# Pooled attention followed by a four-expert attention mixture: q loaded by partition groups and turned by VectorE, first scores on 32-row tiles, and a new written-out order

## The chip, the cores and the metric

The kernel runs on one core of one Trainium2 chip. The metric is the device time of one execution in microseconds; lower is better. Each time of the kernel before is one execution, and the median of three is given.

## What is computed

Inputs are q, k and v of shape 8 batches x 8 heads x 576 positions x 64, and the weights of four experts. Per batch:

```python
k_p = k.reshape(B, H, 72, 8, D).mean(axis=3)         # pooled by 8: 72 keys
v_p = v.reshape(B, H, 72, 8, D).mean(axis=3)
attn = softmax(q @ k_p.T / sqrt(D)); x = attn @ v_p   # first attention, 8 heads
x = x.transpose(0, 2, 1, 3).reshape(B, S, H * D)      # 576 x 512
logits = x @ w_gate                                   # gate: top 2 of 4 experts
for e in range(4):                                    # second attention, causal
    a = causal_softmax((x @ wq[e]) @ (x @ wk[e]).T / sqrt(64))
    out += gate_weight[e] * (a @ (x @ wv[e]) @ wo[e])
```

## The kernel before, in words

The work of a batch is cut into small steps with one- or two-letter names, and a string SEQ (from L551) lists about a thousand of them in one hand-off order: `name args:batch@bank`, with a trailing `d` where the copy that follows a matrix step runs on VectorE instead of ScalarE, and a trailing `c` where a 128-column stationary operand is cut into four strips of 32 columns (`wide`, `flip`, `strips`, L181 to L194). Each engine runs its own steps strictly in the order of the string. There is no scheduler behind it: a step waits only for its data and for its PSUM bank. PSUM is one tile of 8 banks, and the `@` figure is the bank, fixed in the string.

The steps of the first attention, for batch b:

- `L_k`, `L_q`, `L_v` (`load`, L109): DMAs issued from GpSimd, which cast fp32 to bf16 on the way. k and v come in three chunks each, q in six chunks of 96 positions for all 8 heads, 96 partitions per DMA with runs of 64 elements. There are three buffers of each (NRAW).
- `PK`, `kc`, `KT`, `kt`: pooling of k by a matmul with a 0 and 1/8 matrix, its copy, four PE transposes of 96x128 and their copy, so that kpT holds two heads of 64 rows on the 128 partitions.
- `Q0` to `Q3`, `r0` to `r3` (L246, L251): q is turned by PE transposes. Each Q step flips six 96x128 pieces of two heads into one bank as 128x576 bf16 (line L194), and r copies the bank to the tile qT (line L176). A batch has 24 flips and 4 copies.
- `E0` to `E4`, `e0` to `e4` (L255, L263): the scores. E0 to E3 are two matmuls each, one per head, with 64 rows of the array each and 512 columns, into two adjacent banks; E4 does the last 64 positions of all heads. e is the exp on ScalarE, 96x1024 for a pair of banks (L273).
- `D`, `d`, `x` and `PV`, `vc`, `O`, `o`: sums of the exps by a matmul with ones, their reciprocal as exp(-ln(.)) on ScalarE (L294, L298), pooled v, the weighted sum, and its scaling on VectorE into xT (L317).

The second part, two batches to a tile xT: `P` and `p` are the q and k projections of the experts, with their copies; `V` and `v` the values with the gate logits; `g` the gate; `S` and `s` the scores (64-row tiles, two banks) and their exp (L433); `a` the causal mask on GpSimd (L450); `B`, `bz`, `bg`, `b` the weighted sum, its normalizing and gating; `T` and `t` its PE transposes and copy; `Y` and `y` the output projection, its copy and the DMA out. `span` (L456) says into how many parts B is cut: two for batches 0 to 5, three for the last two.

`W0` to `W4` load the expert weights, `c0` to `c4` put them in order; in the string W0 stands behind the loads of batch 1's k and q. `H` steps are matmuls on zeros (L173) that keep TensorE busy while there is nothing to do; there are 51 of them. `M` sets pads on VectorE.

The loads stand in one FIFO on GpSimd together with the causal masks. The copies of all steps are written by one helper (line L176), nearly all matmuls by another (line L185), and so groups are told apart by their tiles.

TensorE addresses its array in tiles: 128x128 for P, V, B, T, Y and the flips, 64x128 for E and S (two matmuls side by side), 128x32 for PK, PV, D, O and the steps with a `c` (four side by side). Going along the string, the tile shape of TensorE changes 97 times; 80 of the changes come behind the first `P_q0:0`.

Of the kernel before, what the change touches and what calls it, by code (L numbers as in the profile page):

```python
# [21 lines left out]
def kernel(  # L22
# [34 lines left out]
    NQC = S // KR  # L57
# [16 lines left out]
    qraws = bufs(NRAW, [KR, NQC, H, D], BF16, "qraw")  # L74
# [3 lines left out]
    kpTs = bufs(2, [128, NHP, KR], BF16, "kpT")  # L78
    vps = bufs(2, [KR, H, D], BF16, "vp")
    qTs = bufs(8, [128, S], BF16, "qT")  # L80
    etas = bufs(2, [KR, NHP, 2, S], BF16, "eta")
# [27 lines left out]
    def load(b, nm, c):  # L109
        if nm == "q":  # L110
            dst = qraws[b % NRAW][:, c, :, :]
            src = q[b, :, KR * c : KR * (c + 1), :].rearrange("h p d -> p h d")
        else:
            raw, T = (kraws, k) if nm == "k" else (vraws, v)
            dst = raw[b % NRAW][:, c, :, :, :].rearrange("p h t d -> p h (t d)")
            src = T[b, :, 2 * KR * c : 2 * KR * (c + 1), :].rearrange("h (p t) d -> p h (t d)", t=2)
        nc.gpsimd.dma_start(out=dst, in_=src)  # L117
# [107 lines left out]
    def kc(b, bank, dve):  # L225
        copy(dve, kps[b % 2][:], psum[0:KR, bank, :])
# [10 lines left out]
    def KT(b, bank):  # L237
        for hp in range(NHP):
            flip(half_bank(bank)[:, KR * hp : KR * hp + KR],
                 kps[b % 2][:, 128 * hp : 128 * hp + 128])  # L240

    def kt(b, bank, dve):
        copy(dve, kpTs[b % 2][:],
             half_bank(bank)[:, 0 : NHP * KR].rearrange("p (a n) -> p a n", a=NHP))
# [18 lines left out]
    def es(b, bank, dve, hp):  # L263
        eta = etas[b % 2]
        if hp == NHP:
            for hh in range(2):
                nc.scalar.activation(
                    out=eta[:, :, hh, MAIN:S],
                    in_=psum[0:KR, bank + hh, 0 : NHP * TAIL].rearrange("p (a n) -> p a n", a=NHP),
                    func=EXP, scale=ATT_EXP_SCALE,  # L270
                )
        else:
            nc.scalar.activation(  # L273
                out=eta[:, hp, :, 0:MAIN], in_=psum[0:KR, bank : bank + 2, :],
# [3 lines left out]
    def heads(b, g, cols):  # L278
        for i in range(4):
            yield i, 4 * g + i, etas[b % 2][:, 2 * g + i // 2, i % 2, cols]  # L280
# [175 lines left out]
    def span(b, part):  # L456
        if b < B - 2:
# [78 lines left out]
    def z(b, c, queue):  # L536
# [9 lines left out]
    MATRIX = {"PK": PK, "PV": PV, "KT": KT, "Q": Q, "E": Es, "D": Dn, "O": Ov, "V": V, "P": P,  # L546
              "S": Sb, "B": Bv, "T": T, "Y": Y}
    READS = {"kc": (kc, "PK"), "vc": (vc, "PV"), "kt": (kt, "KT"), "r": (r, "Q"), "e": (es, "E"),
# [3 lines left out]
        I:0 L_k0:0 L_k1:0 L_k2:0 J:0 K:0 H19:0@0 PK:0@0 kc:0 H4:0@1 KT:0@0 kt:0 L_q0:0 L_q1:0  # L552
        L_q2:0 L_q3:0 L_q4:0 L_q5:0 H8:0@1 Q2:0@0 r2:0 Q1:0@1 Q3:0@2 r1:0d r3:0 H1:0@3 E2:0@4
        e2:0 Q0:0@1 r0:0 E3:0@2 H5:0@0 E0:0@4 e3:0 L_v0:0 L_v1:0 E4:0@0 L_v2:0 PV:0@6 vc:0d e4:0
# [150 lines left out]
```

## Time and profile before

| what | us |
|---|---|
| median of 3 runs (range) | 167.88 (167.41 to 168.09) |
| span of the profiled execution, first to last instruction | 165.0 |
| median less that span | 2.88 |
| TensorE busy | 157.0 |
| ScalarE busy | 135.0 |
| VectorE busy | 123.8 |
| GpSimd busy, most of it issuing DMAs | 104.9 |

The profiled execution is known by its span alone; what the metric holds beside it (2.88 us) is taken as the same for both kernels. Busy times are unions of instruction spans. A matmul's span includes its way through the array, so that a TensorE that always has the next one in flight shows as busy throughout; the columns that it streams are worked out from starts that follow each other. Instructions of ScalarE and VectorE overlap at their ends by about 0.1 us, so a group's cost on the engine is the distance of the starts, not the mean duration.

### The profile page before, as it was taken

To read this page: it belongs to the slowest core of one execution; us is meant where nothing else is said; L and a number is where in the kernel's file an instruction comes from. 1 tells how busy PE (TensorE), PEld (TensorE's weight loads), DVE (VectorE), ACT (ScalarE), POOL (GpSimd) and SP (SyncE) were. 2 spreads that over 40 slices of the span, in tenths; PEclk is the share of its full clock that TensorE was granted. 3 is DMA by queue.
4 is the path that set the end of the run, shared out by engine and by line. 5 is a ranking of instruction groups with operands and counts; after the bars stand their busy time and mean duration, and the time that the engine had idled before them with its cause. 6 is when DMAs were issued, how large, how long until landed. Compare 5 with 4: busy or idle time off the path is not lost. (4 is left out here: it accounts for less than half of the span.)

```text
span 165.0 us, 6106 instructions
## 1 busy us (share of the span) xinstructions
PE 157.0 (95%) x2463; PEld 93.8 (57%) x2463; DVE 123.8 (75%) x410; ACT 135.0 (82%) x247; POOL 104.9 (64%) x178
## 2 busy tenths in 40 slices
PE   6999988999999999999999999999999999999980
PEld 2344354568557656654754878555647686555730
DVE  1101497589799859976988899998998989779960
ACT  3029758999998999888998997789997999898860
POOL 6999891899999999965959997400140211364100
PEclk9999999999999999999999999999999999999998
DMA  2999999999999999999999999923113043055875
GB/s 22 160 153 171 164 172 178 170 145 139 177 156 173 164 157 148 156 233 217 206 178 226 168 198 83 174 100 86 47 68 127 4 131 127 0 190 195 257 260 191
DMA packets 84204, 25.04 MB, mean 152 GB/s; under 512 B 79312, under 2 KB 79568, under 8 KB 84176
## 3 DMA queue, kind: packets, MB, share of 16 engines
q0 software_dynamic: 78928, 15.21, 110.6%
q1 hardware_dynamic: 5024, 9.05, 15.9%
q8 instruction: 19, 0.31, 0.7%
q10 hardware_dynamic: 224, 0.39, 0.6%
q14 instruction: 9, 0.07, 0.1%
HBM read 30.42 MB, written 9.44 MB: 242 GB/s over the span
## 5 line engine op out<-in xcount | busy, mean ns | idle before, releaser
L433 ACT ACTIVATE etb_97<-psum 128x1024 bf16<-128x1024 f32 x24 | 23.6, 1023 | 2.5 <-PE psum L185 2.4
L433 ACT ACTIVATE etb_98<-psum 128x1024 bf16<-128x1024 f32 x24 | 23.5, 1027 | 1.3 <-PE psum L185 1.1
L450 POOL TENSOR_SCALAR_AFFINE_SELECT etb_98<-etb_98 128x256 bf16<-128x256 bf16 x32 | 12.5, 410 | 17.4 <-ACT etb_98 L433 17.2
L450 POOL TENSOR_SCALAR_AFFINE_SELECT etb_97<-etb_97 128x256 bf16<-128x256 bf16 x32 | 12.4, 415 | 15.8 <-ACT etb_97 L433 15.7
L173 PE MATMUL psum<-warm 128*128 128x512 bf16 x51 | 15.2, 443 | 1.8 <-DVE onesd L146 1.3
L273 ACT ACTIVATE eta_91<-psum 96x1024 bf16<-96x1024 f32 x16 | 15.9, 1018 | 1.1 <-PE psum L185 1.1
L273 ACT ACTIVATE eta_92<-psum 96x1024 bf16<-96x1024 f32 x16 | 15.6, 1020 | 0.7 <-PE psum L185 0.6
L117 POOL DMA_DIRECT2D qraw_68<-in_q_dram x18 | 13.9, 775 | 1.2 <-PE psum L185 1.1
L176 DVE COPY ofin<-psum 128x512 f32<-128x512 f32 (+1 forms) x18 | 11.9, 673 | 3.2 <-PE psum L185 2.4
L117 POOL DMA_DIRECT2D qraw_69<-in_q_dram x18 | 13.8, 770 | 0.5 <-issue 0.5
L176 DVE CAST qk_99<-psum 128x512 bf16<-128x512 f32 (+1 forms) x16 | 10.5, 670 | 3.8 <-PE psum L185 3.6
L176 DVE CAST qk_100<-psum 128x512 bf16<-128x512 f32 (+1 forms) x16 | 10.5, 654 | 3.5 <-PE psum L185 3.5
L176 ACT COPY ofin<-psum 128x512 f32<-128x512 f32 (+1 forms) x19 | 10.7, 580 | 2.7 <-PE psum L185 1.8
L185 PE MATMUL psum<-wvg,xT_96 128*32 128x260 bf16 (+1 forms) x120 | 10.8, 275 | 0.0
L173 PEld LDWEIGHTS <-warm 128*128 128x128 bf16 x51 | 5.1, 111 | 9.5 <-issue 5.8
L185 PE MATMUL psum<-wvg,xT_95 128*32 128x260 bf16 (+1 forms) x156 | 10.5, 275 | 0.0
L185 PEld LDWEIGHTS <-etb_97 128*128 128x128 bf16 x240 | 8.8, 97 | 2.0 <-issue 0.4
L117 POOL DMA_DIRECT2D qraw_70<-in_q_dram x12 | 9.2, 784 | 0.0
L185 PEld LDWEIGHTS <-etb_98 128*128 128x128 bf16 x240 | 8.3, 97 | 1.4 <-issue 0.8
L185 PE MATMUL psum<-qk_100 64*128 64x64 bf16 (+4 forms) x96 | 8.8, 276 | 0.1
L117 POOL DMA_DIRECT2D kraw_71<-in_k_dram x9 | 7.0, 787 | 2.7 <-DMA qraw_70<-in_q_dram 1.8
L185 PE MATMUL psum<-qk_99 64*128 64x64 bf16 (+4 forms) x96 | 8.4, 277 | 0.0
(198 smaller groups left out, 452.8 us busy)
## 6 DMA issues: line engine op xcount, KB each, us to landing
out_dram<-ofin SPq DMA_DIRECT2D x31, 256.0 KB, 3.0
kraw_71<-in_k_dram POOLq DMA_DIRECT2D x9, 192.0 KB, 6.2
qraw_68<-in_q_dram POOLq DMA_DIRECT2D x18, 96.0 KB, 5.3
vraw_74<-in_v_dram POOLq DMA_DIRECT2D x9, 192.0 KB, 5.5
kraw_72<-in_k_dram POOLq DMA_DIRECT2D x9, 192.0 KB, 5.9
qraw_69<-in_q_dram POOLq DMA_DIRECT2D x18, 96.0 KB, 5.5
vraw_75<-in_v_dram POOLq DMA_DIRECT2D x9, 192.0 KB, 4.9
kraw_73<-in_k_dram POOLq DMA_DIRECT2D x6, 192.0 KB, 6.5
```

What stands on the lines that cost most here:

```text
L117: nc.gpsimd.dma_start(out=dst, in_=src)
L173: nc.tensor.matmul(out=psum[:, bank, :], lhsT=warm[:, 0:128], rhs=warm[:], start=True, stop=True)
L176: (nc.vector.tensor_copy if dve else nc.scalar.copy)(out=out, in_=in_)
L185: nc.tensor.matmul(out=out, lhsT=lhsT, rhs=rhs, start=start, stop=stop)
L273: nc.scalar.activation(out=eta[:, hp, :, 0:MAIN], in_=psum[0:KR, bank : bank + 2, :], func=EXP, scale=ATT_EXP_SCALE,)
L433: nc.scalar.activation(out=et[:, ep, :, eo : eo + n], in_=psum[:, bank : bank + 2, 0:n], func=EXP, scale=MOE_EXP_SCALE,)
L450: nc.gpsimd.affine_select(out=blk, in_=blk, pattern=[[0, 2], [1, 128]], compare_op=ISGE, fill=0.0, base=0, channel_multiplier=-1,)
```

## The change

- q of one batch is loaded by four DMAs, each to 32 partitions: partition group i takes heads 2i and 2i+1 (g = 0, 1), a partition holds pairs of neighbouring positions, and the runs are 128 elements long. For batch 0 each is cut in two by g, so eight DMAs, and those of g = 0 come first.
- The Q and r steps are gone. `u0` and `u1` (`turn`) turn q by a VectorE transpose of 32x32 blocks, SBUF to SBUF, on pairs of bf16 seen as one fp32: 128x576 such pairs in one instruction, two instructions per batch. After it a partition group of 32 holds one head of the group, a partition holds two neighbouring elements of the head's 64, and the two stand next to each other for each position.
- The scores E are made on tiles of 32 rows and 128 columns: for g = 0 and 1, four heads side by side into four banks, in two accumulating passes (the even and the odd elements), the moving operand read with a step of two elements. E0 and E1 are the 512 columns of g = 0 and 1, E2 the rest of both. An E step now takes two pairs of banks (`E0:0@02` is banks 0 to 3), and two exps of the same size as before follow it (`e00`, `e01`). k is pooled and flipped with its columns reordered to match.
- `span` cuts B into three parts for the first two batches too: 40 B steps for 36, 32 T steps for 24.
- No step has a `c` any more. The tile shape changes 114 times along the string, 105 of them behind the first `P_q0:0`, and 34 warm-up matmuls are left of 51.
- The string is new. The first two weight loads stand behind batch 0's v, ahead of batch 1's loads; batch 0's projections come ahead of batch 1's scores. More copies run on ScalarE (5 weight orderings for 1, 14 p for 8, 14 t for 3, 23 y for 18; fewer of kt, 2 for 5, v, 11 for 14, and kc, 4 for 5).

The core of the diff:

```diff
-    qraws = bufs(NRAW, [KR, NQC, H, D], BF16, "qraw")
+    qraws = bufs(NRAW, [128, 2, NQB, 2, D], BF16, "qraw")
...
-    def load(b, nm, c):
+    def load(b, nm, c, g=None):
         if nm == "q":
-            dst = qraws[b % NRAW][:, c, :, :]
-            src = q[b, :, KR * c : KR * (c + 1), :].rearrange("h p d -> p h d")
+            i, gs = c, slice(0, 2) if g is None else slice(g, g + 1)
+            dst = qraws[b % NRAW][32 * i : 32 * i + 32, gs].rearrange("p g a t d -> p g a (t d)")
+            src = q[b].rearrange("(i g) (a p t) d -> i p g a (t d)", g=2, a=NQB, t=2)[i][:, gs]
...
     def KT(b, bank):
-        for hp in range(NHP):
-            flip(half_bank(bank)[:, KR * hp : KR * hp + KR],
-                 kps[b % 2][:, 128 * hp : 128 * hp + 128])
+        for j in range(4):
+            g, par = j // 2, j % 2
+            flip(half_bank(bank)[:, KR * j : KR * j + KR],
+                 kps[b % 2][:, 256 * g + par : 256 * g + 256 : 2])
...
-    def Q(b, bank, hp):
-        for c in range(NQC):
-            flip(half_bank(bank)[:, KR * c : KR * (c + 1)],
-                 qraws[b % NRAW][:, c, 2 * hp : 2 * hp + 2, :].rearrange("p h d -> p (h d)"))
-
-    def r(b, bank, dve, hp):
-        copy(dve, qTs[4 * (b % 2) + hp][:], half_bank(bank)[:, 0:S])
+    def turn(b, g):
+        src = qraws[b % NRAW][:, g].rearrange("p a t d -> p (a t d)").bitcast(FP32)
+        dst = qTs[b % 2][:, g].rearrange("p s t -> p (s t)").bitcast(FP32)
+        nc.vector.transpose(out=dst.rearrange("p (a s n) -> p a n s", s=32, n=2),
+                            in_=src.rearrange("p (a n d) -> p a n d", n=2, d=32))
...
-    def Es(b, bank, hp):
-        for i in range(NHP) if hp == NHP else [hp]:
-            c0, n, at_ = (MAIN, TAIL, TAIL * i) if hp == NHP else (0, MAIN, 0)
-            for hh in range(2):
-                r0 = hh * D
-                mm(psum[0:KR, bank + hh, at_ : at_ + n], kpTs[b % 2][r0 : r0 + D, i, :],
-                   qTs[4 * (b % 2) + i][r0 : r0 + D, c0 : c0 + n])
+    def four(pairs):
+        return [pairs[0], pairs[0] + 1, pairs[1], pairs[1] + 1]
+
+    def Es(b, pairs, g):
+        banks = four(pairs)
+        for j in range(2) if g == 2 else [g]:
+            c0, n, o = (MAIN, TAIL, TAIL * j) if g == 2 else (0, MAIN, 0)
+            for par in range(2):
+                for i in range(4):
+                    rows = slice(32 * i, 32 * i + 32)
+                    mm(psum[0:KR, banks[i], o : o + n], kpTs[b % 2][rows, j, par, :],
+                       qTs[b % 2][rows, j, c0 : c0 + n, par], start=(par == 0), stop=(par == 1))
...
     def span(b, part):
-        if b < B - 2:
+        if 2 <= b < B - 2:
...
     SEQ = """
+        I:0 L_k0:0 L_k1:0 L_k2:0 J:0 K:0 M:0 L_q00:0 L_q10:0 H8:0@0 L_q20:0 L_q30:0 L_q01:0 L_q11:0 L_q21:0 PK:0@0
+        L_q31:0 H3:0@1 L_v0:0 kc:0 KT:0@0 L_v1:0 u0:0 H2:0@1 kt:0 L_v2:0 E0:0@02 W0:0 H7:0@4 e01:0 W1:0 u1:0 e00:0
+        L_k0:1 E1:0@24 E2:0@06 L_k1:1 e21:0 e10:0 L_k2:1 e20:0 L_q0:1 D0:0@2 e11:0 PV:0@3 L_q1:1 D2:0@0 d0:0 D1:0@1
+        vc:0d L_q2:1 H1:0@4 x0:0 c0:0 O01:0@3 L_q3:1 d1:0 O00:0@2 O20:0@4 o01:0 O10:0@5 x1:0 O11:0@6 L_v0:1 H8:0@1
+        o00:0 d2:0 x2:0 L_v1:1 o11:0 o10:0 L_v2:1 c1:0 P_q0:0@5 L_k0:2 c2:0 o20:0 c3:0 L_k1:2 P_k0:0@4 p_q0:0 L_k2:2
+        P_t0:0@6 p_k0:0 PK:1@5 L_q0:2 p_t0:0 S00:0@0 L_q1:2 kc:1 S03:0@2 S01:0@6 s03:0 KT:1@5 L_q2:2 s00:0 S02:0@2
+        kt:1d H5:0@4 L_q3:2 s01:0 u0:1 W2:0 s02:0 u1:1 E0:1@04 W3:0 e01:1 E1:1@26 W4:0 e11:1 L_v0:2 P_k1:0@4 L_v1:2
+        e10:1 D1:1@5 p_k1:0d PV:1@6 L_v2:2 d1:1 P_q1:0@7 vc:1d e00:1 L_k0:3 E2:1@24 O10:1@6 p_q1:0d L_k1:3 x1:1 O11:1@0
+        D0:1@1 e21:1 o11:1 L_k2:3 PK:2@7 e20:1 d0:1 D2:1@2 O01:1@3 o10:1 L_q0:3 O00:1@0 d2:1 O20:1@1 x2:1 S12:0@4 kc:2d
+        x0:1 L_q1:3 o20:1 s12:0 S11:0@6 o01:1 L_q2:3 P_t0:1@1 o00:1 s11:0 S10:0@2 L_q3:3 KT:2@4 u0:2 P_k1:1@0 p_t0:1
+        L_v0:3 kt:2 u1:2 s10:0 P_k0:1@1 L_v1:3 c4:0 p_k1:1 L_v2:3 E1:2@46 p_k0:1d V3:0@2 L_k0:4 e11:2 V2:0@0 v3:0d
+        L_k1:4 V2:1@1 e10:2 v2:0d E0:2@26 v2:1d L_k2:4 V1:0@0 e01:2 L_q0:4 V0:0@1 v1:0d P_q0:1@4 e00:2 L_q1:4 v0:0d
...
```

More of the change, by code (lines that the diff above doesn't have):

```diff
@@ L56 @@
     KR = 96
[L57 removed]
+    NQB = S // 64
     DSC = 1.0 / 64.0
@@ L263, in es @@
[L263 to L271, printed above, removed]
+        copy(dve, kpTs[b % 2][:].rearrange("p g t n -> p (g t n)"), half_bank(bank)[:, 0 : 4 * KR])
+    def turn(b, g):
[3 more added lines that the diff above has]
+                            in_=src.rearrange("p (a n d) -> p a n d", n=2, d=32))
@@ L272, in es @@
+    def es(b, pairs, dve, g, half):
+        eta, bank = etas[b % 2], pairs[half]
+        if g == 2:
+            nc.scalar.activation(
+                out=eta[:].rearrange("k (i g) s -> k i g s", g=2)[:, 2 * half : 2 * half + 2, :, MAIN:S],
+                in_=psum[0:KR, bank : bank + 2, 0 : 2 * TAIL].rearrange("p i (g n) -> p i g n", g=2),
+                func=EXP, scale=ATT_EXP_SCALE,
+            )
         else:
+            h = 4 * half + g
             nc.scalar.activation(
-                out=eta[:, hp, :, 0:MAIN], in_=psum[0:KR, bank : bank + 2, :],
+                out=eta[:, h : h + 3 : 2, 0:MAIN], in_=psum[0:KR, bank : bank + 2, :],
```

170 lines of the change are left out of this document (70 added, 100 removed).

## The prediction

> **What bounds the kernel now.** I read the page's first two parts, then the busy times in three stretches, and then rows in order of time at the start.
>
> ```profile
> span 165.0 us, 6106 instructions
> ...
> PE   6999988999999999999999999999999999999980
> ...
> DMA  2999999999999999999999999923113043055875
> ...
> 0.00:26.20 26.20, 23.49 (x195) 10.20 (x195) 8.67 (x30) 13.30 (x22) 23.76 (x35) 1.00 1.71 142
> 26.20:160.70 134.50, 133.51 (x2270) 83.66 (x2268) 114.68 (x381) 121.51 (x226) 81.17 (x143) 1.00 1.22 153
> 160.70:165.00 4.30, 0.00 (x0) 0.00 (x0) 0.42 (x1) 0.18 (x1) 0.00 (x0) 0.86 0.55 184
> ```
>
> In a stretch row come its length, then busy time of TensorE, weight loads, VectorE, ScalarE, GpSimd. From 26.2 to 160.7 us TensorE is busy for 133.5 of 134.5 us: it is the bound. ScalarE has 121.5 (90%) and VectorE 114.7 (85%); ScalarE is next, 13 us behind. The first 26 us are another matter: TensorE is busy there too, but much of it with these:
>
> ```profile
> L173 PE MATMUL psum<-warm 128*128 128x512 bf16 x51 | 15.2, 443 | 1.8 <-DVE onesd L146 1.3 <-ACT rza_93 L294 0.5
> ```
>
> So the time is 26.2 us of start, 134.4 of dense TensorE work, and 4.3 from its end to the last DMA; 2.88 more lie between the span and the median of the runs, which I carry over.
>
> **The start.** Rows of the time line, by engine:
>
> ```profile
> 4.05 4.59 POOL L117 DMA_DIRECT2D qraw_68<-in_q_dram  x6
> 12.20 0.73 PE L194 MATMUL psum<-ident,qraw_68 96*128 96x96 bf16 x13 [0.17 <-DMA qraw_68<-in_q_dram]
> 13.60 1.02 ACT L273 ACTIVATE eta_91<-psum 96x1024 bf16<-96x1024 f32 x1
> 20.96 0.72 POOL L130 DMA_DIRECT2D wst_g<-in_moe_w_gate_dram  x1
> 24.46 0.62 ACT L176 COPY wqp_120<-wst_q 128x512 bf16<-128x512 bf16 x1 [1.18 <-DMA wst_q<-in_moe_wq_dram]
> 25.52 1.93 ACT L273 ACTIVATE eta_92<-psum 96x1024 bf16<-96x1024 f32 x2
> 26.23 1.15 PE L185 MATMUL psum<-xT_95,wqp_120 128*128 128x512 bf16 x8
> ```
>
> Six q loads take 0.77 us each on GpSimd, the last issued at 7.9; its data are turned at 12.2, so 4.3 us from issue to use. The first projection starts at 26.23, and its weights were ready only at 25.1, having stood behind batch 1's k and q.
>
> After the change q has eight loads of under half the pieces. Their issue costs between 0.3 us (by size) and 0.77; I take 0.7, since even the 4 KB gate load took 0.72. The fourth (the last of g = 0) is issued at 4.05 + 3 x 0.7 = 6.15, lands at 10.5, and the eighth at 13.3. A turn of 128x576 pairs is not in this trace: from below it is bounded by the copy of 128x576 bf16 (0.45), from above by twice the 128x512 fp32 copy on VectorE (2 x 0.69); I take 0.75, that fp32 copy scaled to 576 columns, because it too moves four bytes per element.
>
> ```profile
> L176 DVE COPY qT_84<-psum 128x576 bf16<-128x576 bf16 x4 | 1.8, 456 | 8.2 <-PE psum L194 8.1
> L176 DVE COPY ofin<-psum 128x512 f32<-128x512 f32 x17 | 11.5, 687 | 2.5 <-PE psum L185 2.4
> L317 DVE TENSOR_TENSOR xT_95<-psum,rza_93 128x512 bf16<-128x512 f32 x8 | 5.1, 680 | 2.1 <-PE psum L185 2.1
> L294 ACT ACTIVATE rza_93<-psum 128x512 f32<-128x512 f32 x8 | 4.8, 596 | 1.2 <-PE psum L185 1.2
> L298 ACT ACTIVATE rza_93<-rza_93 128x512 f32<-128x512 f32 x8 | 5.1, 634 | 0.1
> ```
>
> The first turn ends at 11.3, the first exp starts at 11.9 (13.6 before). The second turn ends at 14.05, so exps of g = 1 and of the tails start at 14.9. ScalarE's instructions overlap: two exps of 1.02 take 1.93 (the row at 25.52), so one costs its duration less 0.11. From 14.9 it has two exps of 1024 (0.91 each), two tails (0.27), two logarithms (L294, 0.49), two exps of them (L298, 0.53) and one weight ordering (0.51): 14.9 + 1.8 + 0.5 + 1.0 + 1.1 + 0.5 = 19.8. Two VectorE products (0.6 apart) and a start follow: the first projection at **21.5**. Its weights, issued behind eight q and three v loads at about 12, are there by 19. Between the issue bounds the start is 19.5 to 22.
>
> **What TensorE no longer does, and what it does more.**
>
> ```profile
> 23.48 1.19 PE L194 MATMUL psum<-ident,qraw_69 96*128 96x96 bf16 x24
> 24.59 0.42 PE L185 MATMUL psum<-qT_87,kpT_80 64*96 64x512 bf16 x2
> 46.39 1.04 PE L185 MATMUL psum<-xT_95,wkp_123 128*32 128x512 bf16 x16
> 47.26 0.23 PE L185 MATMUL psum<-eta_91,onesd 96*32 96x64 bf16 x8
> 47.53 0.60 PE L185 MATMUL psum<-kraw_71,poolk 96*32 96x512 bf16 x6
> 48.07 0.39 PE L185 MATMUL psum<-qk_100 64*128 64x512 bf16 x2
> 48.29 0.38 PE L185 MATMUL psum<-qk_99 64*128 64x64 bf16 x4
> ```
>
> - *Flips of q.* 24 take from 23.48 to 24.59, about 1.15 us with the 64-row step's start. Batches 2 to 7 lie in the dense stretch: -6.9 us.
> - *Scores.* 512 columns cost 0.22 us (48.07 to 48.29, two heads side by side), so four pairs are 0.87 us per batch. On 32 rows it is two passes over two groups of four heads, again four times 512 columns if four run side by side. 128x32 steps do (46.39 to 47.26, 16 matmuls in 0.87 = 4 x 0.22), so 0 us; but these are four column strips that share one moving operand, not four row groups with an operand each and a step of two elements. Bounds: 0, and twice the time (+0.87 per batch).
> - *Tile shape.* Six pooling matmuls, three side by side, are 2 x 0.213 = 0.43 us of columns, and the next shape starts 0.54 after them: 0.11 per change. Behind the first projection there are 105 changes for 80: +2.75 us.
> - *Moved behind the first projection.* Batch 1's pooling (0.45), its k flips (0.18) and two score steps (0.43) were done before 26.2: +1.06.
> - Cutting B and T into more parts changes no column count; cutting by `c` neither (16 strips of 512 cost what 4 wide ones do): 0 on TensorE.
>
> TensorE alone: 21.5 + 134.4 - 6.9 + 2.75 + 1.06 = 152.8 us at its end, for 160.6.
>
> **VectorE** loses 24 copies of qT (24 x 0.45 = 11), gets 16 turns (16 x 0.75 = 12; between the bounds 7 and 22) and gives 11 copies of 0.69 to ScalarE (8). From 115 us in the stretch it goes to 108, at the upper bound to 118, of 131: 0, hidden behind TensorE.
>
> **ScalarE** takes its place. It loses 8 copies of qT and 7 others (8.9 us) and gets 13.0: 4 weight orderings, 6 p, 5 y, 11 t, by rows like those below. To 13.3 + 121.5 + 0.2 = 135.0 come 4.1, so 139.1, of which 10.5 are done by 21.5 (table load and k copies 2.3, exps 4.2, sum steps 3.0, weight orderings 1.0): 128.6 left beside 131.3 of TensorE (152.8 - 21.5). And they are not spread evenly:
>
> ```profile
> L433 ACT ACTIVATE etb_97<-psum 128x1024 bf16<-128x1024 f32 x24 | 23.6, 1023 | 2.5 <-PE psum L185 2.4
> L273 ACT ACTIVATE eta_91<-psum 96x1024 bf16<-96x1024 f32 x16 | 15.9, 1018 | 1.1 <-PE psum L185 1.1
> L176 ACT COPY qT_83<-psum 128x576 bf16<-128x576 bf16 x2 | 1.3, 653 | 0.0
> L176 ACT COPY ofin<-psum 128x512 f32<-128x512 f32 x18 | 10.4, 591 | 2.7 <-PE psum L185 1.8 <-DVE osc_108 L489 0.6 <-DVE oT_112 L176 0.2
> ```
>
> From the first projection to the second exp of batch 2 (`e10:2`) the order gives ScalarE 12 exps of 1024 (0.91: 11.0), 3 of the small ones (0.85), 6 sum steps (2.5), 7 copies (0.28 to 0.48: 2.8) and three weight orderings (2.1, one of them twice as long): 19.3, and with 3% for hand-offs, an estimate, **19.9 us**. TensorE has there 8 projection steps (4 x 0.216 each, the two tails half: 6.1), 3 value steps (1.3), 11 score steps of both parts (3.0), three poolings with two sets of k flips (1.7) and the first attention's sums (1.5), together 13.6, and 17 changes of shape (1.8): **15.4**. TensorE, which must not overwrite a bank before its exp, waits for the difference: **+4.5**. From there ScalarE has 109 beside TensorE's 116, as now: nothing more.
>
> **Loads.** Per batch GpSimd issues 10 DMAs for 12, q in runs twice as long. The DMA digits stay at 9 for 25 slices (103 of 165 us) while TensorE runs dense, so loads don't set its pace now, and they have less to do afterwards: 0. The masks stand behind fewer issues: 0. What that costs if the cover is gone: a batch of loads late by its own length, up to 9 us (12 x 0.77) once.
>
> **Sum.** 152.8 + 4.5 = 157.3, span 161.6, time **164.5** (-2.0%).
>
> **The rivals.**
>
> 1. *ScalarE doesn't bind*: TensorE works ahead on other banks while exps queue. 152.8 + 4.3 + 2.9 = **160.0**. For it: before, ScalarE ran at 90% and cost TensorE 1 us of 134. Against: in the first 18 us the order has little else ready than batch 0's and 1's scores. Chance 0.2.
> 2. *Four row groups don't quite run side by side.* If they reach three quarters of it, 0.22 becomes 0.29: +0.28 per batch, six batches outside the stretch that ScalarE sets, +1.7: **166.2**. Chance 0.12. The Trainium skill states this (TensorE: Matmul & The Clock Gate, Measured speedup vs the span model: 3.07 for four row tiles of 512 columns); no run here shows it yet, and the four column strips above run at 4.0.
> 3. *The moving operand with a step of two streams at half the rate*, so that the change trades flips for streaming: +0.87 x 6 = +5.2: **169.7**. No row has such a step on that side. Chance 0.08.
> 4. *Four banks at once*, the slower end. A score step needed two free banks of 8; now it needs four, the scores of the experts need two, and two are left for all else. TensorE is strictly in order, so it stands until the slowest of the four is read, up to one exp (0.91). Behind the first stretch there are five batches with three such steps. Half an exp at each is 15 x 0.45 = 6.8: **171.3**; it turns the change into a loss from 0.23 us per step on. For it: from now on ScalarE, who empties these banks, is nearly full. Against: the order has its banks laid out by hand. Chance 0.18. The Trainium skill names the pressure (TensorEngine Tiling, Restrictions and Gotchas), without a price.
>
> **Numbers.** Forecast 0.42, its own range 162.5 to 167; rivals 0.2, 0.12, 0.08, 0.18. About 0.5% (167.0 to 168.7) can be told from no change. Faster: nearly all of forecast and rivals 1 and 2, 0.66; same 0.09; slower, rivals 3 and 4, 0.25. The range leaves out the ends of rivals 1 and 4: 158.5 to 170.5.
>
> **What would show it.** Start: first projection at 21 to 22 us, first exp near 12, first turn 0.7 to 0.8 us. Flips: no qraw row on TensorE. ScalarE: over 95% busy from 20 to 42 us with TensorE's waits on exps there, and TensorE full from 45 on. Rivals 2 and 3: a score step of eight matmuls takes 0.43 us to the next start, 0.58, or 0.87. Rival 4: waits of TensorE for eta, spread over all batches. I am wrong if the first projection is later than 24, if TensorE's waits behind 45 us sum to over 4 us, or if VectorE is the releaser of most of them.

## The result, and the profile after

The changed kernel is slower: **177.68 us** median of four runs (175.94 to 180.99) beside 167.64 for the kernel before in the same session, a ratio of 1.058 (95% interval 1.052 to 1.064). The forecast was 164.5 with a range to 170.5, so sign and size were both missed. The profiled execution has a span of 176.2 us. All ratios below are to the kernel before on the same chip; they leave out runs in which the chip was disturbed, and where a median of few runs and a ratio differ the ratio is the one to read.

The first view is the page of the changed kernel, with the rows that answer to those of before.

```profile
span 176.2 us, 5231 instructions
...
PE   7288798998950899999999999999999999989960
...
PEclk9957999999998589999999999999999999999999
DMA  3999999999999998999999921002011020169894
```

Each digit is a fortieth of the span, 4.4 us. In the row of TensorE look at the pair 5, 0 in the twelfth and thirteenth place: between 48 and 57 us the engine that is to be full stands still, and in the row of the granted clock 8, 5, 8 stand from the thirteenth place on. From the 15th slice on TensorE is at 9 but for one slice, until the end. So there is one hole, a thin start, and a dense remainder as before. The busy times by stretch say the same; the columns are those of the same view of before.

```profile
0.00:23.66 23.66, 16.74 (x126) 6.00 (x126) 7.32 (x25) 10.84 (x18) 18.85 (x31) 0.86 1.35 130
23.66:45.00 21.34, 19.53 (x230) 9.64 (x230) 11.62 (x25) 20.43 (x35) 14.91 (x22) 1.00 1.79 181
45.00:65.00 20.00, 13.36 (x153) 7.56 (x153) 10.93 (x42) 10.57 (x24) 16.60 (x30) 0.83 1.73 171
65.00:171.70 106.70, 104.05 (x1526) 60.65 (x1526) 95.55 (x316) 98.55 (x182) 42.41 (x86) 1.00 0.72 130
```

From 45 to 65 us TensorE has 13.4 us of 20 and a clock of 0.83; the dense stretch has 104 of 106.7. What it waited for stands in the view of waits: engine, tile and line, then for whom, microseconds in total, times, the longest.

```profile
PE psum L186 <- POOL etb L454: 6.6, 1, 6.6
```

A single wait of 6.6 us, for GpSimd's causal mask on etb (L454). The time line of TensorE shows where, and that of GpSimd what GpSimd did meanwhile:

```profile
50.04 1.04 PE L186 MATMUL psum<-xT,wqp 128*128 128x512 bf16 x4
57.66 0.76 PE L186 MATMUL psum<-vaug,etb 128*128 128x65 bf16 x6 [6.58 <-POOL etb L454]
```

```profile
44.73 0.77 POOL L118 DMA_DIRECT2D vraw<-in_v_dram  x1 [0.72 <-PE psum L186]
...
48.61 2.30 POOL L118 DMA_DIRECT2D kraw<-in_k_dram  x3 [0.57 <-PE psum L186]
51.19 2.72 POOL L118 DMA_DIRECT2D qraw<-in_q_dram  x4 [0.28 <-DVE xT L321]
54.61 0.77 POOL L118 DMA_DIRECT2D vraw<-in_v_dram  x1 [0.70 <-DMA vraw<-in_v_dram]
55.68 0.77 POOL L118 DMA_DIRECT2D vraw<-in_v_dram  x1 [0.30 <-issue]
56.45 2.22 POOL L454 TENSOR_SCALAR_AFFINE_SELECT etb<-etb 128x256 bf16<-128x256 bf16 x6
```

`B00:0`, the first weighted sum of batch 0, needs masks that stand in the string behind nine of batch 4's ten loads (from `a02:0` behind `L_v1:4` on). GpSimd does its steps strictly in turn. By the rows these nine loads hold it from 48.04 to 56.45, 8.4 us: 6.6 of it is the issuing itself (2.30, 2.72, 0.77 and 0.77), and 1.9 are waits (0.57, 0.28, 0.70 and 0.30), for TensorE to free a raw buffer and, ahead of 54.61, for an earlier v load to land. Only then come the masks, at 56.45. The chain of waits names the same road, from the landing of a v load (6.77 us) to the masks and to TensorE, with two issues of 0.5 and 0.8 us in the part left out. Of the 6.77 us of that landing GpSimd itself stood still for only 0.70; in the rest it was issuing the loads ahead.

```profile
47.27 6.77 DMA vraw<-in_v_dram
...
56.82 1.15 POOL etb L454 x3
...
58.01 4.41 PE psum L186 x34
```

The rest of what the prediction asked for, first three groups by line (busy time, mean of one in ns, idle time before them and what ended it), then rows of the time line of TensorE:

```profile
L251 DVE STREAM_TRANSPOSE qT<-qraw 128x576 f32<-128x576 f32 x16 | 12.0, 765 | 5.4 <-DMA qraw<-in_q_dram 5.4
...
L186 PE MATMUL psum<-eta,onesd 96*32 96x512 bf16 (+1 forms) x128 | 9.2, 290 | 1.5 <-ACT eta L277 1.4
```

```profile
L186 PE MATMUL psum<-qT,kpT 32*96 32x512 bf16 (+1 forms) x256 | 13.7, 312 | 0.6 <-ACT etb L437 0.6
```

```profile
9.33 1.01 PE L186 MATMUL psum<-kraw,poolk 96*32 96x512 bf16 x4 [2.41 <-DMA kraw<-in_k_dram]
...
12.84 1.09 PE L186 MATMUL psum<-qT,kpT 32*96 32x512 bf16 x8
...
23.66 1.02 PE L186 MATMUL psum<-xT,wqp 128*128 128x512 bf16 x4
...
70.00 0.66 PE L186 MATMUL psum<-qT,kpT 32*96 32x512 bf16 x8
70.59 0.60 PE L186 MATMUL psum<-vaug,etb 128*128 128x65 bf16 x14
...
168.96 1.46 PE L186 MATMUL psum<-wop,oT 128*128 128x256 bf16 x8
```

The turn takes 0.765 us (0.75 was taken), and no step of TensorE reads qraw any more. For eta, the exps of the first scores, TensorE waits twice in the whole kernel, 1.7 us in all by its view of waits; 1.4 of it is one wait in the start, at 18.3 us. The 256 matmuls of the score steps, the third group, stand 0.6 us in all for their banks. The first projection starts at 23.66, not 21.5. A score step in the dense stretch takes 0.59 us to the next start (70.00 to 70.59). The last matmul ends at 170.4, 5.8 us ahead of the end of the span; before it was 4.3.

The difference between forecast and result in four parts:

| part | forecast | measured | difference |
|---|---|---|---|
| first projection | 21.5 | 23.66 | +2.2 |
| from there to the end of the last matmul | 135.8 | 146.8 | +11.0 |
| from there to the end of the span | 4.3 | 5.8 | +1.5 |
| outside the span (median less span) | 2.9 | 1.5 | -1.4 |
| time | 164.5 | 177.7 | +13.2 |

The row "outside the span" is no saving. Every execution on record lies 1.7 to 1.9 us above its own span (177.88 for 176.2 in this one); the forecast's 2.9 and the 1.5 here set a median beside the span of an execution that was faster or slower than the median.

### The profile page after: what moved, and what is told of

It reads as the page before. It is cut to its first block, busy times and chain, and to the rows that moved or that the text cites. A ratio compares the mean times of both kernels' runs of the same rounds, so it can differ in the third digit from the quotient of the medians.

```text
span 176.2 us, 5231 instructions
## 1 busy us (share of the span) xinstructions
PE 153.7 (87%) x2028; PEld 83.9 (48%) x2028; DVE 125.4 (71%) x404; ACT 140.4 (80%) x257; POOL 92.8 (53%) x166
## 4 chain that ended last, share of the span: by engine, by line
PE 60%; ACT 12%; DVE 10%; DMA 7%; issue 4%; POOL 2%; ACTq 0%; DVEq 0%; POOLq 0%
PE psum L186 54%; DMA vraw<-in_v_dram 4%; DMA kraw<-in_k_dram 4%; PE psum L195 3%; ACT etb L437 3%; ACT eta L277 3%; PE psum L174 3%; DVE ofin L177 2%; ACT rza L302 2%; ACT rza L298 2%; DVE qk L177 1%; POOL kraw L118 1%; DVE osc L493 1%; DVE gt L488 1%; POOL vraw L118 1%
## 5 line engine op out<-in xcount | busy, mean ns | idle before, releaser
L437 ACT ACTIVATE etb<-psum 128x1024 bf16<-128x1024 f32 x48 | 46.8, 1032 | 1.8 <-PE psum L186 1.4
L454 POOL TENSOR_SCALAR_AFFINE_SELECT etb<-etb 128x256 bf16<-128x256 bf16 x64 | 25.0, 409 | 39.6 <-ACT etb L437 39.0
L277 ACT ACTIVATE eta<-psum 96x1024 bf16<-96x1024 f32 x32 | 31.1, 1022 | 2.5 <-PE psum L186 2.3
L186 PE MATMUL psum<-vaug,etb 128*128 128x65 bf16 x480 | 21.1, 195 | 7.2 <-POOL etb L454 6.6
L118 POOL DMA_DIRECT2D qraw<-in_q_dram x36 | 23.3, 655 | 5.2 <-DMA vraw<-in_v_dram 1.6
L186 PE MATMUL psum<-wvg,xT 128*128 128x260 bf16 x144 | 22.0, 285 | 0.6 <-ACT wvg L177 0.5
L321 DVE TENSOR_TENSOR xT<-psum,rza 128x512 bf16<-128x512 f32 x32 | 20.6, 682 | 1.5 <-ACT rza L302 1.3
L186 PE MATMUL psum<-wop,oT 128*128 128x512 bf16 (+1 forms) x74 | 20.1, 373 | 0.2 <-DVE qk L177 0.2
L186 PE MATMUL psum<-xT,wkp 128*128 128x512 bf16 (+1 forms) x128 | 19.4, 286 | 0.3 <-ACT eta L277 0.3
L186 PE MATMUL psum<-xT,wqp 128*128 128x512 bf16 (+1 forms) x128 | 19.5, 286 | 0.1
```

The lines of the kernel that those rows point to most:

```text
L186: nc.tensor.matmul(out=out, lhsT=lhsT, rhs=rhs, start=start, stop=stop)
L277: nc.scalar.activation(out=eta[:, h : h + 3 : 2, 0:MAIN], in_=psum[0:KR, bank : bank + 2, :], func=EXP, scale=ATT_EXP_SCALE,)
L321: nc.vector.tensor_tensor(out=xT[:, 2 * g + t, mcols(b)], in0=psum[:, bank, :], in1=rz[:, g, 0:MAIN], op=MULT)
L437: nc.scalar.activation(out=et[:, ep, :, eo : eo + n], in_=psum[:, bank : bank + 2, 0:n], func=EXP, scale=MOE_EXP_SCALE,)
L454: nc.gpsimd.affine_select(out=blk, in_=blk, pattern=[[0, 2], [1, 128]], compare_op=ISGE, fill=0.0, base=0, channel_multiplier=-1,)
```

## The experiments

The theory after the trace: the masks behind the loads cost the 6.6 us, and the low clock behind the hole some more. The rival: the masks only show that the whole is late. Open was besides what the +4.5 us that the forecast gave to ScalarE really were, and what the removal of the flips is worth. All edits of the string only move steps unless it is said otherwise.

| kernel | median us | ratio (95% interval) |
|---|---|---|
| after, as changed | 177.7 | 1.058 (1.052 to 1.064) |
| e1: seven masks of batch 0 earlier | 171.0 | 1.022 (1.016 to 1.029) |
| e2: warm-ups in the hole | 175.6 | 1.045 (1.040 to 1.050) |
| e4: e1, nine copies to VectorE | 171.7 | 1.020 (1.013 to 1.027) |
| e6: all masks behind their exps | 169.0 | 1.012 (1.008 to 1.016) |
| e7: e6, 19 warm-ups at the start | 170.2 | 1.014 (1.009 to 1.019) |
| e11: e6 without two weight loads | 168.3 | 1.006 (1.002 to 1.009) |
| e12: e11, nine copies to VectorE | 167.8 | 1.002 (0.998 to 1.005) |
| e16: e6 without 20 loads of q | 168.3 | 1.006 (1.003 to 1.008) |
| e17: e6, second exps halved | 168.5 | 1.005 (1.002 to 1.009) |
| e18: e12, 19 warm-ups at the start | 168.3 | 1.001 (0.997 to 1.005) |
| e19: e6, copies and warm-ups | 169.7 | 1.009 (1.005 to 1.013) |
| e20: e18, e16 and e17 together | 165.7 | 0.989 (0.985 to 0.994) |
| e5: before, two weight loads earlier | 169.7 | 1.012 (1.008 to 1.015) |
| e9: before without flips of batches 2 to 7 | 165.9 | 0.992 (0.989 to 0.995) |
| e10: before without strips | 171.6 | 1.024 (1.020 to 1.027) |
| e13: e9, second exps halved | 165.5 | 0.987 (0.982 to 0.992) |
| e14: before, second exps halved | 167.5 | 1.001 (0.998 to 1.004) |
| e15: e9 without 36 loads of q | 164.8 | 0.985 (0.982 to 0.989) |

One per cent is 1.7 us; two rows that differ by less than half of that can hardly be told apart.

### The masks (e1, e6) and the clock behind the hole (e2)

e1 hands seven masks to GpSimd ahead of batch 4's loads; e6 puts every mask of batches 0 and 1 right behind its exp; e2 leaves the masks and fills the hole. The three edits below stand in the order e1, e2, e6, and of e6 one line of the string is shown.

```diff
-V3:0@2 L_k0:4 e11:2
+V3:0@2 a02:0 a00:0 a01:0 a12:0 a11:0 a10:0 a03:0 L_k0:4 e11:2
```

```diff
-o11:2 B00:0@1 V4:1@0
+o11:2 H24:0@1 B00:0@1 V4:1@0
```

```diff
-S03:0@2 S01:0@6 s03:0 KT:1@5 L_q2:2 s00:0 S02:0@2
+S03:0@2 S01:0@6 s03:0 a03:0 KT:1@5 L_q2:2 s00:0 a00:0 S02:0@2
```

> The changed kernel with batch 0's seven causal masks moved in the order string from behind the loads of batch 4 (k, q and two of v) to ahead of them; all else as it is. Theory A (the masks queue behind loads in GpSimd's one FIFO, TensorE stands 6.6 us for them and restarts at a low clock): the one long wait of TensorE at 51 us goes, the clock stays at 1.0 after 25 us, time about 169 (177.7 less 6.6 and about 2 for the clock). Rival B (four banks or ScalarE would hold TensorE there anyway, the mask only comes last): another wait takes its place, time 175 or more.

> The changed kernel with 24 matmuls on zeros put ahead of the step that waits for the masks (5 us of work, shorter than the wait), so that TensorE is busy in the wait. It splits theory A's two parts: if the low clock after the wait costs time by itself, the clock stays at 1.0 and the time is about 175.7, 2 us less; if it costs nothing (the work after the wait is set by ScalarE), 177.7.

> The changed kernel with every causal mask of batches 0 and 1 handed to GpSimd directly behind the exp that it masks, so ahead of all later loads (e1 moved only seven masks of batch 0). Theory (the masks stand behind load issues that are held up): the second mask wait of 2.06 us in e1 goes too, and nothing takes its place: 168.9 us (168.3 to 169.7), no wait of TensorE for etb over 0.5 us. Rival (GpSimd has no room: each mask ahead of a load delays that load, and TensorE or VectorE then wait for batch 3 to 5 instead): 171 or more, with new waits for kraw, qraw or vraw behind 45 us.

e1 gave back 3.6% (1.058 to 1.022), 6.0 us, or 6.65 between the medians. That is about the size of the wait, and the rival, which asked for 175 or more, is out. The theory had asked for about 169, with the clock, and 171.0 came. The missing 2 us are there to see: in e1 a second wait of the same kind is left, for batch 1's masks behind its loads; the row is from e1's time line of TensorE.

```profile
61.85 0.78 PE L186 MATMUL psum<-vaug,etb 128*128 128x65 bf16 x12 [2.06 <-POOL etb L454]
```

e6 takes it away as well: 169.0, the forecast of its theory to 0.1 us, and in its view of waits TensorE no longer waits for a mask. GpSimd had the room, as its time line in e6 shows: the masks, 0.4 us each, pass between the load issues from 28 us on, while in the changed kernel they began at 56.

```profile
28.02 0.45 POOL L446 TENSOR_SCALAR_AFFINE_SELECT etb<-etb 64x256 bf16<-64x256 bf16 x1
28.40 0.66 POOL L118 DMA_DIRECT2D qraw<-in_q_dram  x1
29.06 0.42 POOL L454 TENSOR_SCALAR_AFFINE_SELECT etb<-etb 128x256 bf16<-128x256 bf16 x1
...
44.12 0.42 POOL L454 TENSOR_SCALAR_AFFINE_SELECT etb<-etb 128x256 bf16<-128x256 bf16 x1
```

e2 filled the hole with 24 matmuls on zeros. The masks came hardly earlier (TensorE goes on with `B00:0` at 56.69 us, 57.66 before), but the clock did not fall, and 1.3% came back, 2.2 us with an error of about 1.4; the theory asked for 175.7, and 175.6 was measured:

```profile
45.00:65.00 20.00, 17.69 (x180) 9.41 (x175) 12.42 (x46) 11.69 (x26) 17.32 (x32) 1.00 1.73 171
```

So a hole of 6.6 us costs about 2 us more by the clock that it loses. The rows behind the hole say the same: from `B00:0` to the next flips of k (57.66 to 62.23 us) the changed kernel takes 4.57 us at a granted clock of 0.50, and e1 takes 2.37 for the same steps (49.32 to 51.69), 2.2 less. The Trainium skill has half the clock after at least one idle window of some 3.4 us (TensorE: Matmul & The Clock Gate, Part 1: The HAM clock gate); the granted clock of 0.83 over 45 to 65 us here and 1.00 in e2 agrees.

With the masks mended the changed kernel is still 1.2% slower than before. From here on that is the question.

### The first 45 us: ScalarE, loads, start (e4, e5, e7, e11, e12, e18, e19)

```diff
-c2:0 o20:0 c3:0
+c2:0d o20:0 c3:0d
...
-p_k0:0 PK:1@5 L_q0:2 p_t0:0
+p_k0:0d PK:1@5 L_q0:2 p_t0:0d
...
-kc:1
+kc:1d
```

e4 does this to nine copies of e1 (c2, c3, c4, p_k0, p_t0 and p_k1 of batch 0, p_t0 and kc of batch 1, kt of batch 2), and e12 to those of e11.

> The first of these kernels, and besides nine copies of batches 0 to 2 between the first projection and 45 us moved from ScalarE to VectorE (weight orderings c2, c3, c4; p and kc, kt of that stretch). Theory (ScalarE sets the pace from 24 to 45 us, 4.5 us over TensorE's own work): 3 us less than with the masks alone, about 166. Rival (the stretch is set by the arrival of loads or by TensorE): the same as with the masks alone, 169.

e4 gave 0.5 us by the ratios, with an error of about 1.5, and nothing by the medians. ScalarE's rows had looked like a bound: in the chain of waits of e6 it holds the road for most of 14 us.

```profile
27.14 1.94 ACT etb L437 x2
29.08 2.73 ACT eta L277 x3
...
38.22 0.93 ACT etb L437
39.15 1.05 ACT wvg L177 x2
```

In e4, with these copies gone, the same stretch of the chain consists of loads:

```profile
14.67 9.02 DMA kraw<-in_k_dram
...
28.95 7.86 DMA qraw<-in_q_dram
...
38.05 10.08 PE psum L186 x114
```

The plainest reading is the stretch that the forecast gave to ScalarE, from the first projection to the end of `e10:2`. Here it is in the changed kernel and then in e4, with the columns as before:

```profile
23.66:43.70 20.04, 18.23 (x220) 8.70 (x220) 10.62 (x21) 19.14 (x34) 14.32 (x21) 1.00 1.79 181
```

```profile
21.98:41.64 19.66, 18.01 (x217) 8.30 (x218) 14.43 (x32) 15.20 (x23) 14.22 (x21) 1.00 1.80 181
```

ScalarE has 3.9 us less to do, and the stretch is 0.4 us shorter. So ScalarE's busy time does not set its length, and the next experiments ease the loads. e5 is the other side of it, the kernel before with the first two weight loads taken from their place behind batch 1's k and q and put ahead of batch 1.

```diff
-L_v2:0
+L_v2:0 W0:0 W1:0
```

> The kernel before with one part of the change alone: the first two weight loads stand right behind batch 0's v instead of behind batch 1's k and q. Theory (the change's early weights bring nothing by themselves, since TensorE's written order has batch 1's scores ahead of the projections, and batch 1's k and q come 1.8 us later): 168 to 170. Rival (the projections at 26.2 waited for the weights): 166.5 to 167.

That alone costs 1.2%, 1.9 us: batch 1's k comes later, and its pooling, one row before, falls into three with waits.

```profile
19.93 0.38 PE L185 MATMUL psum<-kraw,poolk 96*32 96x512 bf16 x1
22.02 0.38 PE L185 MATMUL psum<-kraw,poolk 96*32 96x512 bf16 x1 [1.72 <-DMA kraw<-in_k_dram]
23.08 0.59 PE L185 MATMUL psum<-kraw,poolk 96*32 96x512 bf16 x4 [0.68 <-DMA kraw<-in_k_dram]
```

e11 and e12 leave these two loads out and fill the tiles with zeros:

```diff
     def setup_pads():
+        for nm in ("q", "k"):
+            nc.vector.memset(wst[nm][:], 0.0)
...
-E0:0@02 W0:0 H7:0@4 e01:0 W1:0 u1:0
+E0:0@02 H7:0@4 e01:0 u1:0
```

> e6 (all masks of batches 0 and 1 directly behind their exps, 169.0 us) without the two loads of the q and k weights, 512 KB that stand ahead of batch 1's loads; zeros take their place, so the experts' q and k projections run on zeros. The first batches' loads come 2.9 us earlier (512 KB by 175 GB/s). Theory (between 22 and 45 us ScalarE and the loads both run at their limit, so that relieving one shows the other): little, 168.3 us (167.6 to 169.0). Rival 1 (the loads alone set the pace there): 166.5 or less. Rival 2 (neither: it is the latency of short chains): 169.0.

> e11 with nine copies of the first 45 us moved from ScalarE to VectorE, the same nine that by themselves gave at most 0.6 us from e1 to e4. Theory (ScalarE and the loads both at their limit): relieving both gives what neither gave alone, 166.3 us (165.5 to 167.2). Rival 2 (latency of short chains, not throughput): no less than 168.3. Rival 1 (the loads alone): the same as e11.

e11 gave 0.7%, e12 another 0.4%, no more than the copies gave without it. My theory, that ScalarE and the loads hide each other, asked for 166.3 from e12. 167.8 was measured, which isn't that gain; the rival of short hand-offs asked for 168.3 or more and isn't met either. The start was tried in e7, with 19 warm-ups ahead of the first pooling:

```diff
-H8:0@0
+H19:0@0
```

> e6 with 19 matmuls on zeros at the start instead of 8, as the kernel before has. Theory (the granted clock between 10 and 20 us, 0.74 in the changed kernel, costs at the start): first pooling and first scores at full speed, the first E step 0.6 us for 1.03, the first projection 0.4 to 0.8 us earlier than in e6, and as much off the time. Rival (the start is a chain of loads, turns and exps that TensorE's clock hardly touches): within 0.3 us of e6.

Here is TensorE's time line in e6, and then in e7, at the first scores and the first projection; of e6 also the last matmuls:

```profile
12.23 1.09 PE L186 MATMUL psum<-qT,kpT 32*96 32x512 bf16 x8
...
22.44 1.02 PE L186 MATMUL psum<-xT,wqp 128*128 128x512 bf16 x4
...
159.36 1.46 PE L186 MATMUL psum<-wop,oT 128*128 128x256 bf16 x8
```

```profile
10.91 0.65 PE L186 MATMUL psum<-qT,kpT 32*96 32x512 bf16 x8 [0.43 <-DVE qT L251]
...
20.83 1.02 PE L186 MATMUL psum<-xT,wqp 128*128 128x512 bf16 x4
```

The first scores took 0.65 for 1.09 us, and the projection came at 20.83, ahead of the forecast's 21.5. The time did not follow: 1.014 for 1.012, with an error of about 1.1 us on the difference. In the two profiles the last matmul ends at 160.8 in e6 and 160.2 in e7, so of the 1.6 us at the first projection 0.6 were left at the end. The full 1.6 us is out; the 0.4 to 0.8 that the theory asked for lies within the error.

> e12 (masks behind their exps, no loads of the q and k weights, nine copies moved to VectorE, 167.8 us) with 19 warm-up matmuls at the start as in e7, where the first projection came 1.6 us earlier and the time fell by 0.4 at most. Theory (start, loads and ScalarE take each other's place in the first 45 us): with all three eased the start's 1.6 us come through, 166.2 us (165.5 to 167.0). Rival (hand-offs in the order behind 25 us): 167.4 or more.

> What of the repairs leaves nothing out: masks behind their exps, 19 warm-ups at the start, nine copies moved to VectorE; weight loads as in the changed kernel. Theory (the early loads stay in place of what was eased): 168.3 us (167.5 to 169.0), so no better than the kernel before. Rival (start and copies add up): 167 or less.

All three eased at once (e18) come to 1.001, or 167.2 us. That lies between the theory (167.0 or less) and the rival (167.4 or more), and the executions differ: of the eight in the ratio, the two with a granted clock of 0.993 and 0.994 over the whole execution took 166.2 and 166.0 us, the six with 0.983 to 0.990 took 167.2 to 168.5. So neither is shown. e19, which leaves no work out, is 0.9% slower than the kernel before, as its theory asked; none of the mended versions that do all the work beats the kernel before.

### Behind 45 us (e16, e17, e20)

e16 drops the loads of q for batches 3 to 7 from e6's string, e17 reads half of what the second part's exps read in batches 2 to 7, e20 has everything at once.

```diff
-                out=et[:, ep, :, eo : eo + n], in_=psum[:, bank : bank + 2, 0:n],
+                out=et[:, ep, 0 : 1 + (b < 2), eo : eo + n], in_=psum[:, bank : bank + 1 + (b < 2), 0:n],
```

> e6 (the changed kernel with its masks directly behind their exps, 169.0 us) without the 20 loads of q for batches 3 to 7; their scores are made with q of batches 0 to 2. Theory (hand-offs and ScalarE hold it back, the loads only in the first 45 us, which this run leaves as they are): 168.7 us (168.0 to 169.3). Rival (loads hold it back behind 45 us too): 167.3 or less.

> e6 with the exps of the second part halved in batches 2 to 7 (one bank of the two is read), which takes 15 us from ScalarE behind 45 us, where it is 93 to 97% busy in e6. Theory (ScalarE holds TensorE back behind 85 us: the wait of 1.2 us at 94 and the 2 us at the end): 166.5 us (165.8 to 167.5). Rival (ScalarE is full because nothing presses it; the waits are hand-offs): 168.5 or more.

> e18 without the 20 loads of q for batches 3 to 7 (their scores use q of batches 0 to 2) and with the second part's exps halved in batches 2 to 7: start, early loads, later loads and ScalarE all eased at once. Theory (throughput of these takes turns as the bound): close to what TensorE has to do, 163 us (162 to 164.5). Rival (hand-offs of the fixed order, which no throughput mends): 165.3 or more.

e16 and e17 gave 0.7% each, 1.1 us with an uncertainty of about 0.8. For e16 the time, 168.3, lies in the theory's range, though the gain is more than the 0.3 us that it took, and the rival (167.3 or less) is out; e17, at 168.5, comes close to its rival and is far from its theory (167.5 or less), so that the exps don't hold TensorE by much. e20 is at 0.989, 2.3% below e6: 3.9 us in all, as 1.9 (e18) and twice 1.1 add up, within the error, and none hides another. But even there, with some 14 us less for ScalarE (halving the exps took 13.6 in e14) and 22 loads fewer, TensorE takes from its first projection at 20.77 to the end of its last matmul at 157.16

```profile
20.77:157.16 136.39, 133.91 (x1903) 76.57 (x1902) 119.65 (x389) 111.17 (x229) 59.36 (x114) 1.00 0.85 128
```

136.4 us, where the forecast for TensorE alone was 131.3 (152.8 - 21.5). The 5 us that are left are not throughput of ScalarE, nor the loads that were taken away. About half of them, 2.5 us (136.4 less 133.9), is time in which TensorE stands; the other 2.6 is busy time above the 131.3. Some of that may be the flips, whose removal took 4.0 us of busy time in e9 below, not 6.9; no run separates it.

### What the flips were worth (e9, e13, e14, e15), and the change of shape (e10)

e9 is the kernel before with the steps Q and r of batches 2 to 7 struck out of its string, so that q of these batches isn't turned. e15 drops also their loads of q; e13 and e14 halve the second part's exps as e17 does, e14 with the flips left in.

> The kernel before without the Q and r steps of batches 2 to 7 (144 flips, 24 copies); the scores of these batches are made with q of batches 0 and 1, so q's turning is left out for six batches. Theory (TensorE is the bound behind 26 us and a batch of flips costs 1.15 us there, as the forecast took): 6.9 us less, 160.8 (160.2 to 161.8). Rival (ScalarE and VectorE, at 90 and 85%, or the loads, take over as soon as TensorE has less to do): 163 to 166.

> e9 (the kernel before without q's flips in batches 2 to 7, 165.9 us for the 160.8 that the flips' 6.9 us ask for) with the exps of the second part halved in these batches (one bank of the two is read, the other half of the weights stays as it was), which takes 36 x 0.43 = 15 us from ScalarE. Theory (without the flips ScalarE, at 90%, is the next bound, and holds back 5 of the 6.9 us): 161.5 us (160.8 to 163). Rival (loads, VectorE's copies and short hand-offs of a string that was laid out around the flips): 164.5 or more.

> The kernel before with the same halved exps of the second part in batches 2 to 7, flips left as they are: the control to e13. Theory (with the flips TensorE is the bound from 26 us on): no change, 167.3 us (166.7 to 167.7). Rival (TensorE's full row hides waits for ScalarE already in the kernel before): 165.5 or less.

> e9 (the kernel before without q's flips in batches 2 to 7, 165.9 us) and without the 36 loads of q for these batches, which nothing reads there. Theory (the DMAs, busy to 103 us of 165, set the pace as soon as TensorE has less to do): 162 us (161 to 163), and no wait of TensorE for kraw, vraw or wop. Rival (hand-offs of 0.3 to 0.6 us between engines in a string that was laid out around the flips): no less than 165.

This is the second surprise. 144 flips, priced at 6.9 us of TensorE, were gone, and the time fell by 0.8%, 1.4 us. The stretch behind the first 26 us, beside the one of before, shows it:

```profile
26.20:160.00 133.80, 129.50 (x2128) 77.43 (x2124) 108.95 (x362) 119.62 (x222) 81.09 (x143) 1.00 1.22 153
```

TensorE is busy for 129.5 of 133.8 us, so gaps have come up; before, it was 133.5 of 134.5. Its busy time fell by 4.0 us, not by 6.9. Since a matmul's span includes its way through the array, gaps shorter than that don't show as idle; or the flips cost less than the forecast's price. No run separates the two. The control e14 agrees that ScalarE wasn't the bound as long as the flips were there: 13.6 us less of its busy time changed nothing (1.001, within 0.3%). e13 gives 0.5%, 0.9 us with an error as large, to ScalarE (0.987 for 0.992), and e15 0.6%, 1.1 us, to the loads (0.985). What TensorE waits for in e9 behind the first 30 us is a list of small items:

```profile
PE psum L185 <- DMA wop<-in_moe_wo_dram: 0.9, 1, 0.9
PE psum L185 <- ACT kpT L176: 0.6, 2, 0.4
PE psum L194 <- DVE osc L489: 0.4, 2, 0.2
PE psum L185 <- DVE ofin L176: 0.3, 1, 0.3
```

The Q steps stood in the string between steps of which some still wait for a copy or an exp. I read it so that they cost TensorE time that it could hardly use otherwise in that order; no run isolates this.

> The kernel before without the flag that cuts 128-column operands into strips: the same columns, 134 changes of the tile shape instead of 97. Theory (a change costs TensorE 0.11 us, as the forecast took): +37 x 0.11 = +4.1, 171.8 (170.8 to 172.8). Rival (a change is hidden behind the weight load, and only the sums of the forecast put 0.11 on it): 167.7, or less, since 34 steps have a quarter of the weight loads.

e10 strikes the trailing `c` from 34 steps of the kernel before: 134 changes of shape for 97. 2.4% (2.0 to 2.7) of 167.3 us is 3.9 us, or 0.107 us per change; 0.11 was the forecast's price.

## Why the prediction was wrong

**The step that failed** is "The masks stand behind fewer issues: 0." It counted the issues of a batch, 10 for 12. What a mask waits for are the loads that stand in the string between its exp and itself, and these became more: for the seven masks of batch 0 that e1 moves they are 2 to 20 in the kernel before and 12 to 28 in the changed one, 2 to 18 in e1 and none in e6. Before, `B00:0` stands behind q of batch 3; after, behind v of batch 4. The nine loads of batch 4 alone took 8.4 us, 6.6 of it issuing and 1.9 waiting. The wait, its smaller sequel and the clock behind the hole are what e6 gives back: 1.058 to 1.012, 4.6% or 7.6 us. So the term put at 0 makes up more than half of the 13.2 us. In the two profiles the stretch behind the first projection falls from 146.8 to 138.4 us, 8.4, and the start differs by another 1.2, since the landing of k's chunks varies (TensorE waits 3.7 us in all for them in the changed kernel and 2.7 in e6). By the prediction's own signs, waits behind 45 us of over 4 us in sum would show it wrong; this one alone is 6.6. The prediction named "a batch of loads late, up to 9 us" as the price of lost cover, and did not look at what stands behind the loads in the same queue. The string gave that order away: the masks of batch 0 behind `L_v1:4`, and `B00:0` twenty steps on.

**"Batches 2 to 7 lie in the dense stretch: -6.9 us"** is the second miss, and enough by itself for the sign. As time it is not that: e9 measured -1.4 in the order of before. By the profiles 2.9 of the 6.9 us are busy time that the removal didn't take away (4.0 for 6.9), and 3.3 came up as gaps (4.3 us for 1.0). Loads are about 1 us of it (e15), ScalarE 0.9 with an error as large (e13); the remainder I read as short hand-offs, from the list of waits, and it was not isolated.

**ScalarE, +4.5.** The number came out by luck: the stretch took 20.0 us for the forecast's 19.9, but not for that reason. ScalarE was 96% busy there (19.14 of 20.04 us), as forecast, and with 3.9 us of its work moved away (e4) the stretch was still 19.7; the time gained 0.5 us (e4) or 0.6 (e12). The busy share was read as a bound. I take it for a chain of dependent steps, projection, copy, score, exp, with little other work between them in the first batches, and for loads; no run isolates that.

**Loads, 0.** Wrong by 1 to 2 us: putting two weight loads ahead of batch 1 costs 1.9 us in the order of before (e5), leaving them out of the changed one gives 1.1 (e11), and leaving out q's later loads 1.1 (e16).

**The start, 21.5.** 23.66 was measured: k's third chunk landed late (the wait of 2.41 us at 9.33), and with 8 warm-ups the granted clock was 0.69 from 5 to 14 us, and the first scores took 1.09 us (0.65 in e7). With 19 warm-ups it was 20.83, but most of that was gone by the end: 0.6 of 1.6 us in the profiles, nothing that the ratios show (e7).

**Right** were the turn (0.765 for 0.75), the price of a change of shape (0.107 for 0.11, e10), and VectorE at no cost, since it releases no long wait of TensorE. The score step on 32 rows, costed at 0.43 and a change, 0.54, took 0.59: +0.05 for 14 steps behind the first projection, 0.7 us.

**The rivals.** Rival 1 (ScalarE doesn't bind) was right about ScalarE, and wrong that 160.0 would follow. Rival 2's sign was 0.58 to the next start, and 0.59 was measured, but with a change of shape in it. Where the next step has the same shape (`E1:0` to `E2:0`, whose first matmuls start at 16.12 and 16.61 us) it is 0.49: between the forecast's 0.43 and the rival's 0.58, and nearer the forecast. Rival 3 asked for 0.87 and is out. Rival 4 is out: it asked for 6.8 us, and the score steps wait 0.6 us in all for their banks. That a queue would stall was not among them.

**The end, 4.3.** 5.8: eight half-width output matmuls come last, and I suppose that their copies and stores pile up. This was not tried, and the cause is open.

So with the masks mended the forecast of 164.5 would have met 169.0, by the profile of e6: the first projection at 22.4 (+0.9), 138.4 us from there to the last matmul's end (+2.6), 5.8 to the end of the span (+1.5), and 2.4 outside it (-0.5). What is left open is what the 5 us of e20 are made of, 2.5 of standing and 2.6 of busy time.

## What to carry to other kernels

When an engine that issues loads also computes, follow its queue step by step across the change: a cheap operation behind loads waits for the issue of each of them and for everything that they wait for. Count the loads between its producer and itself, not those of a batch, and put it right behind its producer. In a fixed order, work struck out of a full engine is a gain only where the next step's inputs are already there; strike it out alone and measure before it goes into a sum. A high busy share isn't a bound until relieving the engine moves the end.

## What the runs showed of the hardware

- Four tiles of 32 rows, each with its own operand read with a step of two elements, run almost fully side by side: 8 matmuls of 512 columns take 0.59 us to the next start with a change of shape in it, and 0.49 without one (16.12 to 16.61), where one behind the other they would take 8 x 0.213 = 1.70. That is a factor of 2.9 with the change and 3.5 without. The Trainium skill gives 3.07 for four row tiles of 512 columns (TensorE: Matmul & The Clock Gate, Measured speedup vs the span model); it lies between the two.
- A load issue on GpSimd costs nearly the same whatever its size: half a q load (72 KB, batch 0) 0.61 us (seven in 4.25), a whole one 0.68 (four in 2.72 at 51.19), a third of v 0.77. The row is from GpSimd's time line in the changed kernel.

```profile
4.07 4.25 POOL L118 DMA_DIRECT2D qraw<-in_q_dram  x7
```

- Halving the second part's exps takes 13.6 us of ScalarE's 135.0 and moves the time of the kernel before by nothing (e14: 1.001, interval 0.998 to 1.004), though ScalarE was at 90% of the dense stretch.
